# One weight load instead of two, and a last row tile that leaves in three pieces of 512, 416 and 96 columns

## The chip, the cores and the metric

The kernel runs on one core of a Trainium2 chip. The metric is the device time of one execution in microseconds (us), outside the profiler. Where the text quotes a profile, its times count from the start of the profiled execution ("span").

## The reference

A pre-norm transformer block on 2048 tokens of width 1024, in bfloat16: sliding-window attention with 32 heads and a window of 256, then a two-layer MLP with SiLU of hidden width 3584, each with a residual.

```python
h = x + attention(layernorm(x), wqkv, window=256) @ wo     # wo: 1024 x 1024
h2 = h + silu(layernorm(h) @ w1) @ w2                      # w1: 1024 x 3584, w2: 3584 x 1024
```

## The kernel before

The block is worked through in four blocks of 512 tokens. TensorE runs almost without a pause (busy for 690.1 of 695.5 us): while the scores of one block are made, it computes the projections of the next. Two places matter here. The first is where the attention output weights `wo` are loaded: into a buffer that held eight tiles of x, in two halves, at the start of the stage that projects the last block (b = 3).

```python
    r_o = big.tile([P, 8192], BF16, name="r_o")
    x_ring = [view(r_o, i * 1024, 1024) for i in range(8)]     # tiles of x, two blocks
    wo = view(r_o, 0, KT, D)                                   # the same bytes, later
    # ... for b in range(2, NB): ...
        else:                                                  # the last block
            nc.sync.dma_start(out=wo[:, 0:4, :], in_=wo_v[:, 0:4, :])
            nc.sync.dma_start(out=wo[:, 4:8, :], in_=wo_v[:, 4:8, :])
            load_res(0)
            load_res(1)
```

The second is the MLP's second matmul. Each row tile of 128 tokens is a sum over 28 tiles of the hidden width (FT = 28), in pieces of columns. Each piece has a PSUM bank, is evicted by one VectorE operation that adds the residual, and leaves by its own DMA. All row tiles have two pieces of 512 columns; the very last has four, so that little is left to do behind the last matmul.

```python
        for j in range(4):
            cols = [(0, 512), (512, 1024)]
            if b == NB - 1 and j == 3:
                cols = [(0, 512), (512, 768), (768, 896), (896, 1024)]
            accs = [next_acc() for _ in cols]
            # ...
            for acc, (c0, c1) in zip(accs, cols):
                mm2(acc, j, c0, c1, early, FT)                 # 28 matmuls
                nc.vector.scalar_tensor_tensor(out=t_out[j % 2][:, c0:c1], in0=acc[:, 0:c1 - c0], scalar=0.5,
                                               in1=t_in[j % 2][:, c0:c1], op0=ALU.mult, op1=ALU.add)
                nc.sync.dma_start(out=out2d[(b * 4 + j) * P:(b * 4 + j + 1) * P, c0:c1], in_=t_out[j % 2][:, c0:c1])
                # ... steps of the next block's layer norm in between ...
```

The softmax here doesn't subtract the row's maximum and nothing guards it: scores larger than these inputs give would overflow.

## Time and profile before

| | before |
|---|---|
| time, median of 3 (and of 6 once the change was timed) | 696.75 us (696.72 us) |
| spread of the 6 | 696.40 to 697.18 us |
| span of the profiled run | 695.5 us |
| TensorE busy | 690.1 us, 99% |
| last matmul's end to the end of the span | 2.8 us |

The lines that carry this are in the prediction. One more belongs here. It is the kernel before's list of waits in its first 8 us, and it is the first wait of the run that depends on a transfer (columns: who waits for what, us in total, times, longest):

```profile
DVE ln_st L169 <- DMA r_o<-in_A_x_dram: 2.8, 1, 2.8
```

The layer norm of the first tile cannot start before that tile is there.

### The profile page before, as it was taken

The page shows a single profiled execution, that of the slowest core. Times are in us where ns is not written, and L with a number is a line of the kernel's source. Part 1 is how long each engine was busy: PE and PEld are TensorE (multiplying, and loading weights), DVE is VectorE, ACT ScalarE, POOL GpSimd, SP SyncE. Part 2 cuts the span into 40 slices and gives each one's busy share as a digit, 9 for nine tenths or more (in the row PEclk, how much of TensorE's full clock was granted, in tenths as well). Part 3 has the DMA queues.
Part 4 walks back from the last instruction along what each step waited for, and adds up shares of the span by engine and source line. Part 5 has one row for each costly group of instructions (what it writes and reads, how often), then busy time and mean ns, then how long its engine had stood idle before and what let it go on. Part 6 is the DMA issues. An engine that isn't in the chain of part 4 may idle for free.

```text
span 695.5 us, 12334 instructions
## 1 busy us (share of the span) xinstructions
PE 690.1 (99%) x5091; PEld 331.6 (48%) x5091; DVE 289.5 (42%) x616; ACT 257.9 (37%) x328; POOL 174.5 (25%) x391
## 2 busy tenths in 40 slices
PE   8999999999999999999999999999999999999998
PEld 3444444555555555544444444444444444444445
DVE  6267646644443448544316134433133251244111
ACT  4326657777777777621310023300033100233000
POOL 1007667777777777500000000000000000000000
PEclk9999999999999999999999999999999999999999
DMA  7732131026231778880123410024200023100110
GB/s 241 257 53 77 35 93 51 17 60 193 70 124 23 205 251 272 199 311 31 31 76 99 107 38 1 1 83 77 83 1 1 11 95 91 45 1 1 30 39 24
DMA packets 76457, 60.84 MB, mean 87 GB/s; under 512 B 50288, under 2 KB 60528, under 8 KB 76400
## 3 DMA queue, kind: packets, MB, share of 16 engines
q1 hardware_dynamic: 76256, 59.78, 29.9%
q8 instruction: 40, 0.66, 0.4%
q10 hardware_dynamic: 144, 0.26, 0.1%
q14 instruction: 17, 0.14, 0.1%
HBM read 39.85 MB, written 8.39 MB: 69 GB/s over the span
## 4 chain that ended last, share of the span: by engine, by line
PE 99%; DMA 1%; DVE 0%; issue 0%
PE hacc L563 19%; PE hacc L600 17%; PE acc L248 16%; PE acc L600 10%; PE acc L563 9%; PE acc L238 8%; PE acc L267 7%; PE o_ps L339 4%; PE sc L285 3%; PE hacc L267 1%; PE o_ps L354 1%; PE sc L313 1%; DMA r_o<-in_A_x_dram 1%; PE tp L216 0%; DVE ln_st L169 0%; DVE r_o L197 0%
## 5 line engine op out<-in xcount | busy, mean ns | idle before, releaser
L330 POOL TENSOR_SCALAR_AFFINE_SELECT r_e<-r_e 128x256 bf16<-128x256 bf16 (+1 forms) x384 | 171.6, 477 | 116.5 <-ACT r_e L322 65.1
L293 ACT ACTIVATE r_e<-sc 128x1024 bf16<-128x1024 f32 x144 | 139.5, 1021 | 45.1 <-PE sc L285 31.0
L600 PEld LDWEIGHTS <-r_a 128*128 128x128 bf16 x952 | 90.9, 98 | 103.0
L563 PEld LDWEIGHTS <-r_w 128*128 128x128 bf16 x896 | 87.4, 98 | 104.8
L600 PE MATMUL hacc<-r_a 128*128 128x512 bf16 (+2 forms) x616 | 122.5, 360 | 0.0
L563 PE MATMUL hacc<-r_e,r_w 128*128 128x512 bf16 x456 | 100.9, 379 | 0.0
L572 ACT ACTIVATE r_n<-hacc 128x512 f32<-128x512 f32 x30 | 17.9, 597 | 178.9 <-PE hacc L563 178.9
L600 PE MATMUL acc<-r_a 128*128 128x512 bf16 x336 | 74.0, 379 | 0.0
L248 PEld LDWEIGHTS <-r_w 128*128 128x128 bf16 x512 | 46.5, 97 | 57.1 <-issue 7.0
L250 DVE CAST r_a<-acc 128x512 bf16<-128x512 f32 x56 | 38.7, 691 | 72.9 <-PE acc L248 56.3
L248 PE MATMUL acc<-r_t,r_w 128*128 128x512 bf16 x256 | 60.0, 379 | 0.0
L248 PE MATMUL acc<-r_w 128*128 128x512 bf16 x256 | 58.2, 380 | 0.0
L267 PE MATMUL acc<-r_o,r_a 128*128 128x512 bf16 x208 | 49.4, 380 | 0.0
L563 PE MATMUL acc<-r_e,r_w 128*128 128x512 bf16 x216 | 49.1, 379 | 0.0
L339 PEld LDWEIGHTS <-r_e 128*128 128x128 bf16 x1152 | 39.5, 96 | 17.0
L322 ACT ACTIVATE r_e<-sc 128x1024 bf16<-128x1024 f32 x36 | 34.9, 1021 | 21.2 <-PE sc L313 20.1
L339 PE MATMUL o_ps<-r_a,r_e 128*128 128x33 bf16 x1152 | 40.2, 178 | 0.0
L615 DVE SCALAR_TENSOR_TENSOR r_t<-hacc,r_t 128x512 bf16<-128x512 f32 (+2 forms) x22 | 14.0, 635 | 56.7 <-PE hacc L600 56.7
L267 PEld LDWEIGHTS <-r_a 128*128 128x128 bf16 x256 | 23.1, 98 | 29.6 <-issue 5.1
L615 DVE SCALAR_TENSOR_TENSOR r_t<-acc,r_t 128x512 bf16<-128x512 f32 x12 | 8.3, 692 | 64.2 <-PE acc L600 64.2
L573 DVE SCALAR_TENSOR_TENSOR r_a<-r_n,hacc 128x512 bf16<-128x512 f32 x30 | 20.6, 688 | 33.0 <-ACT r_n L572 33.0
L563 PE MATMUL hacc<-r_a,r_w 128*128 128x512 bf16 x144 | 32.9, 379 | 0.0
(71 smaller groups left out, 476.5 us busy)
## 6 DMA issues: line engine op xcount, KB each, us to landing
r_w<-in_B_w_dram SPq DMA_DIRECT2D x8, 896.0 KB, 5.1
r_a<-in_B_w_dram SPq DMA_DIRECT2D x7, 1024.0 KB, 7.9
r_w<-in_A_wqkv_dram SPq DMA_DIRECT2D x6, 1024.0 KB, 8.7
h_dram<-r_t SPq DMA_DIRECT2D x16, 256.0 KB, 3.0
r_t<-h_dram SPq DMA_DIRECT2D x16, 256.0 KB, 2.8
out_dram<-r_t SPq DMA_DIRECT2D x31, 128.0 KB, 1.7
r_o<-in_A_x_dram SPq DMA_DIRECT2D x15, 256.0 KB, 4.0
r_e<-h_dram SPq DMA_DIRECT2D x3, 1024.0 KB, 5.7
```

Source lines behind the costliest of these rows:

```text
L238: nc.tensor.matmul(acc, lhsT=lnT_b[b % 2][:, kt, j * P:(j + 1) * P], rhs=wv[:, kt, c * 512:(c + 1) * 512], start=(kt == 0), stop=(kt == KT ...
L248: nc.tensor.matmul(acc, lhsT=wqk[:, kt, col0:col0 + P], rhs=lnT_b[b % 2][:, kt, :], start=(kt == 0), stop=(kt == KT - 1))
L250: copy(out=(qT, kT)[which][b][:, g, :], in_=acc)
L267: nc.tensor.matmul(acc, lhsT=qT[b][:, g, j * P:(j + 1) * P], rhs=wo[:, g, c * 512:(c + 1) * 512], start=(g == 0), stop=(g == G - 1))
L285: nc.tensor.matmul(sc[hh // 2][:, hh % 2, ch * P:(ch + nq) * P], lhsT=kT[t // 4][r0:r0 + DH, g, (t % 4) * P:(t % 4 + 1) * P], rhs=qT[b][r0 ...
L293: nc.scalar.activation(out=e, in_=sc[pair], func=ACT.Exp, scale=scale)
L322: nc.scalar.activation(out=e, in_=sc[pair], func=ACT.Exp, scale=scale)
L330: nc.gpsimd.affine_select(out=ap, in_=ap, pattern=[[0, 2], [0, n], [sgn, P]], compare_op=ALU.is_ge if upper else ALU.is_gt, fill=0.0, base ...
L339: nc.tensor.matmul(o_ps[pair][:, qt * 2 + hh, 0:VW], lhsT=e_of(i, kind, pair)[:, hh, ch * P:(ch + 1) * P], rhs=v[:, b * 4 + kt, g * 4 + pa ...
L563: nc.tensor.matmul(acc, lhsT=w1[:, kt, ft * P:(ft + 1) * P], rhs=ln2T[b][:, kt, :], start=(kt == 0), stop=(kt == KT - 1))
L600: nc.tensor.matmul(acc[:, 0:c1 - c0], lhsT=gT[:, ft, j * P:(j + 1) * P], rhs=w2[ft // 4][:, ft % 4, c0:c1], start=(ft == 0), stop=(ft == F ...
L615: nc.vector.scalar_tensor_tensor(out=t_out[j % 2][:, c0:c1], in0=acc[:, 0:c1 - c0], scalar=0.5, in1=t_in[j % 2][:, c0:c1], op0=ALU.mult, o ...
```

## The change

The intent is one DMA issue less for the weights and, at the end, one piece less, with a smaller last piece.

```diff
-            nc.sync.dma_start(out=wo[:, 0:4, :], in_=wo_v[:, 0:4, :])
-            nc.sync.dma_start(out=wo[:, 4:8, :], in_=wo_v[:, 4:8, :])
+            nc.sync.dma_start(out=wo, in_=wo_v)
@@
             if b == NB - 1 and j == 3:
-                cols = [(0, 512), (512, 768), (768, 896), (896, 1024)]
+                cols = [(0, 512), (512, 928), (928, 1024)]
```

## The prediction

Passages that rested on something else than the traces of this case are cut out of the prediction and of two expectations, at the marks. No term of the prediction's sum is among them: 0.07 + 0.03 + 0.01 = 0.11 us. Three numbers need their source named. The 1.19 us of the last piece are 28 x (96 x 0.415 + 2.5) ns, from the two values worked out there. The "6.1 us with 56 matmuls" are the 6.20 us of the chain less 0.07. The "0.1 to 0.2 us" for a last transfer at double cost is an estimate; the DMA view of the kernel before from 692.5 us on shows the engines busy for 0.5, 0.8 and 0.5 of three slices of 75 ns in this transfer, 0.14 us.

> **What bounds the kernel now.** I read the page's first lines, then its chain that ended last, then the last twenty microseconds by window, by chain and by group, and last the stretch where the attention output weights are loaded.
>
> The page, its span, its first row of busy time and the summary of its chain:
>
> ```profile
> span 695.5 us, 12334 instructions
> PE 690.1 (99%) x5091; PEld 331.6 (48%) x5091; DVE 289.5 (42%) x616; ACT 257.9 (37%) x328; POOL 174.5 (25%) x391
> ...
> PE 99%; DMA 1%; DVE 0%; issue 0%
> ```
>
> The reader is to see one bound: TensorE is busy for 690.1 of 695.5 us and the chain runs over it for 99% of the span. A change elsewhere counts only if it makes TensorE wait, or if it shortens what stands before its first or behind its last matmul. The time outside the profile is 696.75 us, 1.25 us above the profiled span; I carry differences of the span over to it.
>
> The end of the run, in windows cut at the starts of the VectorE operations that evict each piece of the last row tile (512, 256, 128, 128 columns), then what is left. The columns are PE, PEld, DVE, ACT and POOL busy time, granted clock, DMA share and GB/s:
>
> ```profile
> 680.45:686.46 6.01, 6.01 (x30) 2.80 (x29) 0.69 (x1) 0.00 (x0) 0.00 (x0) 1.00 0.06 22
> 686.46:689.55 3.09, 3.09 (x32) 2.79 (x31) 0.69 (x1) 0.00 (x0) 0.00 (x0) 1.00 0.13 45
> 689.55:691.11 1.56, 1.56 (x32) 1.56 (x30) 0.42 (x1) 0.00 (x0) 0.00 (x0) 1.00 0.14 41
> 691.11:692.68 1.57, 1.53 (x28) 1.35 (x25) 0.30 (x2) 0.00 (x0) 0.00 (x0) 1.00 0.15 31
> 692.68:695.50 2.82, 0.00 (x0) 0.00 (x0) 0.29 (x1) 0.00 (x0) 0.00 (x0) 0.87 0.07 12
> ```
>
> Each piece is 28 matmuls (one for each of the 28 tiles of the hidden width); the extra ones in a window's count overlap its edges. TensorE has no gap up to 692.65 us, and then 2.8 us pass without it: one eviction, one DMA issue, one landing and the end of the program. The chain of this stretch in order of time, and the last issue in the timeline:
>
> ```profile
> 686.46 6.20 PE hacc L600 x84
> 692.65 0.02 issue
> 692.68 0.29 DVE r_t L615
> ```
>
> ```profile
> 693.00 0.36 SPq L617 DMA_DIRECT2D out_dram<-r_t  x1
> ```
>
> The evictions by width, in the groups of this stretch (mean ns of one after the bar):
>
> ```profile
> L615 DVE SCALAR_TENSOR_TENSOR r_t<-hacc,r_t 128x512 bf16<-128x512 f32 x1 | 0.7, 692 | 5.4 <-PE hacc L600 5.4
> L615 DVE SCALAR_TENSOR_TENSOR r_t<-hacc,r_t 128x128 bf16<-128x128 f32 x2 | 0.6, 292 | 2.4 <-PE hacc L600 2.4
> L615 DVE SCALAR_TENSOR_TENSOR r_t<-hacc,r_t 128x256 bf16<-128x256 f32 x1 | 0.4, 425 | 2.4 <-PE hacc L600 2.4
> ```
>
> The weights' two loads, in the timeline of the DMA queue, and the first matmul that reads them, in the timeline of all engines:
>
> ```profile
> 163.86 0.58 SPq L496 DMA_DIRECT2D r_o<-in_A_wo_dram  x1
> 165.97 0.39 SPq L497 DMA_DIRECT2D r_o<-in_A_wo_dram  x1
> 166.42 0.96 SPq L256 DMA_DIRECT2D r_a<-in_A_x_dram  x2
> 168.95 8.86 SPq L375 DMA_TRANSPOSE r_a<-r_n  x2
> ```
>
> ```profile
> 229.58 1.68 PE L267 MATMUL acc<-r_o,r_a 128*128 128x512 bf16 x7
> ```
>
> The per-line view gives 5.5 us to landing for the first half and 6.4 us for the second, so the weights are in place at 172.4 us, 57 us before they are used.
>
> [...] 1.56 us / 28 = 55.7 ns at 128 columns [...], 6.01 / 28 = 215 ns at 512 [...]. [...] the timeline has 15 matmuls of 33 columns in 0.53 us, of which 0.178 is the length of the last, so 0.35 / 14 = 25 ns, with a weight load for each. [...] The last piece has 256 B a row now and will have 192 B; the trace shows what 256 B rows cost at this place: 1.5 us from the last issue to its landing, the same 1.5 us as the 64 KB piece with 512 B rows.
>
> **The change part by part.**
>
> *Last row tile, TensorE.* The columns stay 1024, so streaming is the same; what goes is one piece, 28 weight loads and 28 matmuls, and with each matmul its fixed part. From the windows: (215 - 55.7) / 384 = 0.415 ns a column, so the fixed part is 55.7 - 128 x 0.415 = 2.5 ns. 28 x 2.5 = 0.07 us. [...] All of it is on the path: I take 0.07.
>
> *Last eviction.* 425 - 292 = 133 ns for 128 columns and 692 - 425 = 267 for 256: 1.04 ns a column and 158 ns fixed. At 96 columns this is 258 ns against 292: 0.03 us, on the path. The eviction at 416 columns takes 158 + 433 = 0.59 us and lies beside the 1.19 us of the last piece's matmuls. Its DMA issue (0.34 us) follows; 0.59 + 0.34 = 0.93 is still under 1.19 + 0.26 = 1.45, when the last issue is due. So the bigger middle piece stays hidden.
>
> *Last transfer.* 24 KB in place of 32 KB, the same 128 rows. Issue and landing are mostly fixed (1.5 us for 32 KB and for 64 KB), so I count 0.01 us. One eviction and one DMA issue less earlier on are off the path. What follows the landing stays, about 1 us (695.5 - 693.00 - 1.5).
>
> *Attention output weights.* The upper half already waits for the turned input tiles (1.4 us of wait for those transposes in the queue's view); the lower half goes 2.1 us earlier because its part of the buffer is free. In the changed order the one load stands where the first stood and carries the waits of both, so it issues at about 166 us. 2 MB now start there where 1 MB did. The halves took 5.5 and 6.4 us beside other traffic, so the load should land by 173 to 176 us, 50 us or more ahead of use at 229.58. The two residual loads and the next transposes sit behind up to 3 us more of data. The residual tiles are first used at 230 us too; the transposes write operands of that same later stage, and their source is one of three buffers that come round every 7.6 us, so they have over 10 us. SP saves one issue, 0.4 us of an engine that mostly waits. Worth: 0.00.
>
> Sum: 0.07 + 0.03 + 0.01 = 0.11 us of 696.75, or 0.016%. 696.75 - 0.11 = 696.64, which I state as 696.65.
>
> **The rivals.**
>
> *The last transfer gets worse.* Rows of 192 B that begin 1,856 B into a row of the output might cost more than aligned 256 B. [...] Against: 256 B and 512 B rows landed after the same 1.5 us. [...] even at double cost this is an estimated 0.1 to 0.2 us, and would give 696.7 to 696.8: the gain is eaten.
>
> *Something in the way of the last transfer.* The third piece took 2.6 us to land where the last took 1.5; an instruction fetch of 16 KB stood in a DMA queue in that window. Should such a fetch meet the last piece, the end moves by 1.1 us, to 697.7. With 56 TensorE instructions fewer I expect that fetch to fall away instead, with no effect on the end.
>
> *The weights' load delays something on the path.* If the transposes behind it came late enough for VectorE to wait for its buffer, TensorE would stall once by some microseconds: 698 to 700. Against: 10 us of slack by the count above, and no TensorE wait for a DMA in that stage.
>
> *The merged load helps.* One large load instead of two[...]. But TensorE has no wait there to give back: 0.
>
> **Range and chances.** Three runs of before spread over 0.43 us, four times the predicted gain, so the range is that of the runs: 696.65 with some 0.5 us to either side, 696.1 to 697.2. Two per cent are 14 us; faster by that is excluded by what stands outside TensorE's work (some 5 us in all), and slower would need a stall that nothing here suggests: 0.005, 0.99, 0.005.
>
> **What would show it.** The TensorE piece after the 512 columns lasts 6.1 us with 56 matmuls; the eviction of 96 columns takes about 258 ns and that of 416 about 590; from the last issue to the end remain 2.5 us; the load of the weights issues near 166 us, lands before 180, and no TensorE wait appears between 166 and 240 us. It would be wrong if the landing of the last piece took over 1.7 us, if VectorE or SP still held the 416 piece when the 96 columns were ready, or if transposes after 166 us held up VectorE.

## The result and the profile after

| | before | after |
|---|---|---|
| median of 6 runs | 696.72 us | 696.86 us |
| range | 696.40 to 697.18 | 696.58 to 697.20 |
| ratio, 95% interval | | 1.0001, 0.9989 to 1.0014 |
| span of the profiled run | 695.5 us | 694.9 us |

Ratios are the mean time of one kernel's fast runs over that of the other's of the same rounds, so not quite the ratio of the medians. The interval is some 0.9 us to either side; the predicted gain of 0.1 us cannot be seen in it, and neither can a loss of that size. The answer to "was the gain there?" must come from the traces.

The spans differ by 0.6 us in favour of the change, but this is not the change. In the kernel after, the same first wait reads:

```profile
DVE ln_st L169 <- DMA r_o<-in_A_x_dram: 2.3, 1, 2.3
```

and in the two timelines of VectorE, before and then after, the first statistics operation, which ends that wait, starts 0.57 us apart, before anything that was changed:

```profile
4.33 1.29 DVE L169 BATCH_NORM_STATS2 ln_st<-r_o 128x6 f32<-128x512 bf16 x2 [2.84 <-DMA r_o<-in_A_x_dram]
```

```profile
3.77 1.29 DVE L169 BATCH_NORM_STATS2 ln_st<-r_o 128x6 f32<-128x512 bf16 x2 [2.27 <-DMA r_o<-in_A_x_dram]
```

From here on I measure from the start of this operation, which takes the landing out of the comparison, and cut the rest at two events: the last DMA issue and its landing. The views print hundredths; the third decimals here are from the trace's own timestamps.

The end of the kernel after, in windows cut as before at the starts of the evictions (512, 416 and 96 columns, then the rest; columns as in the prediction):

```profile
685.92:690.84 4.92, 4.92 (x33) 2.81 (x32) 0.69 (x2) 0.00 (x0) 0.00 (x0) 1.00 0.08 27
690.84:692.03 1.19, 1.15 (x28) 1.00 (x24) 0.59 (x2) 0.00 (x0) 0.00 (x0) 1.00 0.00 0
692.03:694.90 2.87, 0.00 (x0) 0.00 (x0) 0.26 (x1) 0.00 (x0) 0.00 (x0) 1.00 0.15 46
```

Its chain in order of time, its evictions by width, and its last issue in the timeline:

```profile
685.88 6.13 PE hacc L599 x56
692.01 0.02 issue
692.03 0.26 DVE r_t L614
```

```profile
L614 DVE SCALAR_TENSOR_TENSOR r_t<-hacc,r_t 128x416 bf16<-128x416 f32 x1 | 0.6, 592 | 4.2 <-PE hacc L599 4.2
L614 DVE SCALAR_TENSOR_TENSOR r_t<-hacc,r_t 128x96 bf16<-128x96 f32 x1 | 0.3, 257 | 0.6 <-PE hacc L599 0.6
```

```profile
692.31 0.33 SPq L616 DMA_DIRECT2D out_dram<-r_t  x1
```

The pieces take 4.92 and 1.19 us (175.7 and 42.5 ns a matmul), where the prediction's 0.415 ns a column and 2.5 ns a matmul make 4.90 and 1.19; 6.13 us of TensorE in place of 6.20; 257 ns for the last eviction in place of 292. From the first statistics to the last issue: 688.661 us before, 688.548 after, 0.113 us less. The sum in the prediction up to this point was 0.10 us (0.07 + 0.03).

The load of the weights, in the timeline of the DMA queue after:

```profile
165.40 0.38 SPq L496 DMA_DIRECT2D r_o<-in_A_wo_dram  x1
```

It takes 9.5 us to land by the per-line view, so until 174.9 us.

The last transfer before and after, in the list of DMA issues (size, us from issue to landing):

```profile
out_dram<-r_t SPq DMA_DIRECT2D x1, 32.0 KB, 1.5
```

```profile
out_dram<-r_t SPq DMA_DIRECT2D x1, 24.0 KB, 1.4
```

What follows the last issue did not shrink. It took 2.49 us before and takes 2.56 after, though the landing itself got 0.05 us shorter (1.47 and 1.42 us). So of the 0.11 us gained, some 0.07 were lost again behind the last issue: 0.12 behind the landing, less the 0.05. There the prediction had said that "what follows the landing stays". The closing is a series of waits in both traces: SP passes five semaphore waits, for the same semaphores in the same order (693.40 to 694.68 us before, 692.69 to 693.78 after), then the engines drain and meet (to the end at 695.49 and 694.87 us). The per-line view of the closing has VectorE's drains (least, median and longest ns, first and last start), and the waits of SP there show how long the meeting took. First before, then after:

```profile
L648 DVEq DRAIN  x2: 19/174/330, 692.7 to 695.1; - x2
```

```profile
SPq L648 <- PEq L648: 0.6, 2, 0.4
```

```profile
L647 DVEq DRAIN  x2: 137/216/295, 692.0 to 694.5; - x2
```

```profile
SPq L647 <- PEq L647: 0.9, 2, 0.7
```

The second of VectorE's two drains is the closing one: it takes 137 ns in place of 19, and SP's longest wait in the meeting is 0.7 us in place of 0.4. In the trace this drain starts 0.44 us after the semaphore record before it, where it was 0.09 us.

Some matmul records are missing in the trace after (4976 matmuls on the page, with 5063 weight loads; the page of the kernel before has 5091 of each, 28 more). It doesn't touch these readings.

### The profile page after: what moved, and what is told of

It is laid out like the page before. It is cut to its first block, busy times and chain, and to the rows that moved or that the text cites. A ratio compares the mean times of both kernels' runs of the same rounds, so it can differ in the third digit from the quotient of the medians.

```text
span 694.9 us, 12185 instructions
## 1 busy us (share of the span) xinstructions
PE 685.5 (99%) x4976; PEld 329.8 (47%) x5063; DVE 289.3 (42%) x615; ACT 257.9 (37%) x328; POOL 174.6 (25%) x391
## 4 chain that ended last, share of the span: by engine, by line
PE 99%; issue 1%; DVE 0%
PE hacc L562 18%; PE hacc L599 17%; PE acc L248 16%; PE acc L599 10%; PE acc L562 9%; PE acc L238 8%; PE acc L267 7%; PE o_ps L339 4%; PE sc L285 3%; PE hacc L267 1%; PE o_ps L354 1%; PE sc L313 1%; PE o_ps L165 1%; PE tp L216 0%; DVE r_e L160 0%
## 5 line engine op out<-in xcount | busy, mean ns | idle before, releaser
L599 PEld LDWEIGHTS <-r_a 128*128 128x128 bf16 x924 | 89.0, 98 | 104.8
L248 PE MATMUL acc<-r_t,r_w 128*128 128x512 bf16 x241 | 58.5, 379 | 0.8
L267 PEld LDWEIGHTS <-r_a 128*128 128x128 bf16 x256 | 23.1, 98 | 29.6 <-issue 5.1
```

Of the source, the lines that this page charges most:

```text
L248: nc.tensor.matmul(acc, lhsT=wqk[:, kt, col0:col0 + P], rhs=lnT_b[b % 2][:, kt, :], start=(kt == 0), stop=(kt == KT - 1))
L267: nc.tensor.matmul(acc, lhsT=qT[b][:, g, j * P:(j + 1) * P], rhs=wo[:, g, c * 512:(c + 1) * 512], start=(g == 0), stop=(g == G - 1))
L599: nc.tensor.matmul(acc[:, 0:c1 - c0], lhsT=gT[:, ft, j * P:(j + 1) * P], rhs=w2[ft // 4][:, ft % 4, c0:c1], start=(ft == 0), stop=(ft == F ...
```

## The experiments

Theory A: the terms of the prediction hold up to the last issue, and single runs differ by the landing of the first tile. Theory B: something in the change, not chance (theory C), delays the closing. I read from each trace: first statistics to last issue; issue to landing; landing to the end of the program; and the number of VectorE's records (operations, semaphore records and drains). All in one table, the runs follow one by one. "Late" means that VectorE's closing drain took 136 to 138 ns; in all other traces it took 19. The experiments ran on three chips; wo_at_20, on another one than tail_only, repeats its stretch up to the last issue to the hundredth.

| run | to the last issue | to landing | to the end | VectorE records | drain | ratio to before (95%) |
|---|---|---|---|---|---|---|
| before | 688.66 | 1.47 | 1.02 | 707 | | |
| after | 688.55 | 1.42 | 1.14 | 705 | late | 1.0001 (0.9989 to 1.0014) |
| same_again | 688.55 | 1.43 | 1.13 | 705 | late | 0.9999 (0.9987 to 1.0012) |
| dve_pad | 688.56 | 1.43 | 0.84 | 706 | | 0.9996 (0.9983 to 1.0008) |
| tail_only | 688.54 | 1.44 | 0.96 | 706 | | 0.9997 (0.9983 to 1.0011) |
| wo_only | 688.64 | 1.46 | 0.94 | 706 | | 0.9996 (0.9983 to 1.0008) |
| dve_pad_64 | 688.56 | 1.43 | 0.84 | 765 | | 0.9994 (0.9979 to 1.0009) |
| dve_pad_128 | 688.57 | 1.42 | 0.85 | 829 | | 1.0003 (0.9987 to 1.0020) |
| dve_pad_132 | 689.82 | 1.43 | 1.14 | 833 | late | 1.0003 (0.9986 to 1.0019) |
| eighths | 708.30 | 1.45 | 0.97 | 858 | | 1.0260 (1.0244 to 1.0276) |
| two_pieces | 688.91 | 1.67 | 0.98 | 704 | | 1.0001 (0.9986 to 1.0016) |
| last32 | 688.93 | 1.46 | 1.13 | 705 | late | 1.0008 (0.9993 to 1.0023) |
| wo_at_20 | 688.54 | 1.43 | 0.84 | 706 | | 0.9998 (0.9983 to 1.0013) |
| wo_at_23 | 692.90 | 1.43 | 1.14 | 705 | late | 1.0047 (1.0030 to 1.0063) |

### same_again: the changed kernel once more

No edit.

> The changed kernel once more, unaltered. Theory A (the change is worth 0.11 us up to the last DMA issue; differences of some tenths between single runs come from when the first input tile lands, since the two traces so far differ by 0.57 us there already): from the first layer-norm statistics operation to the last DMA issue 688.55 us again (the kernel before: 688.66), whatever the start is; time within 0.3 us of the kernel before, ratio 0.9995 to 1.0005. Theory B (something in the change costs as much as it gains, since the medians show 696.86 against 696.72): the stretch up to the last issue repeats, and from the last issue to the end of the program takes 2.56 us again, against 2.49 before. Theory C (the closing stretch is chance): this stretch takes another value between 2.3 and 2.7 us.

The first statistics started at 4.40 us this time (3.77 in the trace before it), and everything behind repeated: 688.55 us to the last issue, 2.56 us from there to the end, the drain 138 ns. Its five runs have a median of 696.87 against 696.90 for the kernel before. Theory A holds, and of the other two theory B: the slow closing repeats and is not chance.

### dve_pad: one VectorE instruction more

```diff
     run_late()
     load_w2(5)
+    pad = const.tile([P, 1], F32, name="pad")
+    nc.vector.memset(pad[:], 0.0)
```

> The changed kernel with one tiny VectorE memset (128x1) ahead of the MLP, so that VectorE has as many instructions as in the kernel before (563; the change has 562). In the trace of the changed kernel VectorE's closing drain came 0.4 us after its release and took 137 ns, in the kernel before 0.09 us and 19 ns. If the late drain comes from where VectorE's instruction stream ends (theory B), it is gone here, and from the last issue to the end take about 2.2 us: 2.49 less some 0.2 because the last-landing piece is now also the last one waited for, less some 0.05 for the landing. If it is chance (theory C), this stretch bears no relation to the count. Up to the last issue 688.55 us, as theory A has it. Time: 0.3 us under the changed kernel for theory B, the same for theory C; either is at the edge of the noise.

From the last issue to the end 2.27 us, with the drain on time; the expected value was about 2.2. The per-line view of the closing and the waits of SP:

```profile
L649 DVEq DRAIN  x2: 19/158/297, 692.1 to 694.2; - x2
```

```profile
SPq L649 <- PEq L649: 0.6, 2, 0.4
```

One instruction that does nothing useful took 0.29 us off the closing. The rest of the difference to before (1.02 to 0.84 us behind the landing) has the reason that the expectation gave: SP passes five closing waits, and each one that is already met takes it 0.06 us (in the kernel before the last three start at 694.53, 694.59 and 694.65 us). In the kernel before the last landing ends the second of them, so three follow; in tail_only and wo_only the third; in this kernel and the changed one the fifth. Which one it is goes with the number of DMAs in the program: one DMA less in each part of the change, two in all. In the traces before and after, the DMAs signal eight semaphores in turn; the last of 186 signals one that SP's second closing wait asks for, the last of 184 one of the fifth. I read this order in the traces and did not vary it by itself.

### tail_only and wo_only: one part of the change each

tail_only is the kernel before with the three pieces alone, wo_only the kernel before with the single load alone.

> The kernel before with the last row tile in three pieces alone; the weights in two loads. Theory A: the whole gain is here: 688.55 us from the first statistics to the last issue, as in the changed kernel. Rival (merging the loads gave part of the 0.11 us): 688.6 or more. Time within 0.3 us of the kernel before.

> The kernel before with the single weight load alone; the last tile in four pieces. Theory A: nothing: 688.66 us from the first statistics to the last issue, as in the kernel before; the load issues near 166 us and lands before 176. Rival: any difference of 0.03 us or more there would be the merged load's. From the last issue to the end 2.49 us as before if that stretch depends on the program (it has before's VectorE count and tail), other values if it is chance.

688.54 us and 688.64 us to the last issue: the gain of 0.11 us is in the tail, and wo_only is only 0.02 us under the kernel before, below the 0.03 us that I had set as the least to be called a difference. The single load in wo_only was issued at 165.6 us and landed 9.5 us later.

The closing is quick in both, 2.40 us from issue to end. For wo_only I had expected 2.49 as before; most of the difference is the one closing wait fewer behind the last landing. For tail_only it is a surprise, since its trace has as many VectorE operations as the changed kernel's (615; the kernel before has 616; the 562 and 563 in the expectation of dve_pad stand in no trace). So my explanation by the count of operations needed a correction: what counts are all records. The tail removes one eviction (707 to 706), the merged load one semaphore record of VectorE's (707 to 706), and only both together reach 705, where the drain is late. Neither part alone has the loss.

### dve_pad_64, dve_pad_128 and dve_pad_132: does 705 come round?

The expectation of the first two was that 128 more instructions would bring the late drain back and 64 would not. The 128 was my estimate; no trace up to then showed it.

```diff
             silu(b, acc, ft)
+            if 1 <= b <= 2 or b == 3 and ft < 8:
+                nc.vector.memset(pad[:], 0.0)          # 64 in all; twice each for 128
```

> The changed kernel with 64 tiny VectorE memsets spread over the MLP. What is to be told apart: the closing drain of VectorE was late (137 ns, some 0.35 us after it was due) in both traces with 705 VectorE records and in none with 706 or 707. Theory B (the late drain belongs to a place in the instruction stream that comes round with the 8 KB instruction fetches[...]): with 769 records it is not late, and from the last issue to the end take 2.27 us as with one memset. Theory B' (what matters is only having more instructions than 705): the same here. Up to the last issue 688.55 us in either; a slower MLP would show that the memsets themselves cost something.

> The same with 128 memsets, 833 VectorE records if none is added beside them. Theory B (period of 128): the closing drain is late again and from the last issue to the end take 2.56 us. Theory B': not late, 2.27 us. Theory C (chance): either. Up to the last issue 688.55 us.

Neither was late, but the second did not test what it was meant to. Four semaphore records fell away where the memsets were put, so it had 829 records and not 833. With four memsets more at the last of these places:

> The changed kernel with 132 tiny VectorE memsets in the MLP. The run with 128 of them gave 829 VectorE records and not the 833 (705 + 128) that its expectation named, as four semaphore records fell away (with 64 memsets, too: 765); so the period of 128 has not been tried. This one should have 833. The late closing drain came in all four traces with 705 records and in none with 704, 706, 707, 765, 829 or 858. Theory B (a place in the stream that comes round every 128 instructions, with the 8 KB fetches): late, and from the last issue to the end 2.56 us. Theory B' (705 is late for another reason): not late, 2.27 us. Up to the last issue 688.55 us.

833 records, and the drain is late: 138 ns, 2.56 us from issue to end.

```profile
L652 DVEq DRAIN  x2: 138/218/297, 694.2 to 696.6; - x2
```

That is 705 + 128, as theory B had it. Its 689.82 us to the last issue missed the expectation by 1.3 us, and this belongs to the start of that one run: its first 15 us had a granted clock of 0.89 (0.50 from 7.8 to 11.2 us) and 11.73 us of TensorE, the changed kernel's 1.00 and 13.39. It was the slowest of its four runs (698.72 us, the others 696.47 to 697.12).

The traces have 8 KB instruction fetches (DMA queue q14 of the page: 17 packets in the kernel before, 16 in the changed one). How many instructions one of them brings is not shown.

The times of these fetches go with a place in VectorE's stream. In the nine traces with 704, 705 or 706 records the last one starts 1.11 to 1.13 us after the end of VectorE's record number 703; in dve_pad_132 it starts as long after number 831, which is 703 + 128. The record behind that place, number 704 or 832, is the late one: it starts 0.44 to 0.46 us after the one before it, where a drain in the closing is otherwise 0.09 us behind. With 705 and 833 records this is the closing drain, and the whole meeting waits for it (SP's longest wait there is 0.7 us in place of 0.4). With 704 (two_pieces) it is VectorE's very last semaphore record, which comes 0.115 us after that of SP; in all other traces it comes 0.01 us after. With 706 it is a semaphore record that starts 1.7 to 1.9 us later, when the meeting of the engines begins, so that the step is hidden.

So the place is shown, and that it comes round after 128 records by one run. What takes the time in the step is not shown: the fetch itself starts 0.53 to 0.55 us after the late drain has ended, so the drain did not wait for that fetch, and no record says what it waited for.

### eighths: the fixed cost of a matmul, made large

```diff
+            elif b > 0 or j > 0:
+                cols = [(c, c + 128) for c in range(0, D, 128)]
```

> The kernel before with 14 of the 15 row tiles of the MLP's second matmul after the first, and the last but for its own four pieces left alone, in eight pieces of 128 columns in place of two of 512; so 14 x 6 x 28 = 2352 more matmuls and weight loads over the same columns. Theory A (each matmul has a fixed 2.5 ns and its weight load is hidden): 2352 x 2.5 ns = 5.9 us more up to the last issue, 694.5 us, and a time 5.9 us over the kernel before, ratio 1.0084. [...] Rival (the fixed part is hidden or an edge effect of the last tile): under 2 us more.

The expectation failed: 19.6 us more and not 5.9 up to the last issue, and 1.026 in time. But the fixed cost itself is as expected. In the last block, where no layer norm of a next block lies between, TensorE runs on (busy for all 37 us from 660 to 697), and VectorE's timeline has a piece of 128 columns every 1.563 us (24 evictions; two of them):

```profile
690.42 0.29 DVE L617 SCALAR_TENSOR_TENSOR r_t<-acc,r_t 128x128 bf16<-128x128 f32 x1 [1.27 <-PE acc L600]
691.98 0.29 DVE L617 SCALAR_TENSOR_TENSOR r_t<-acc,r_t 128x128 bf16<-128x128 f32 x1 [1.27 <-PE acc L600]
```

1.563 us / 28 = 55.8 ns a matmul with its weight load, over 36 us; four such pieces are 0.21 us more than one of 512 columns (6.04 us), which is 84 times 2.5 ns. So 5.9 us of the 19.6 are this. The rest is something I had not looked for: the three earlier blocks. The waits of TensorE and of VectorE between 360 and 660 us:

```profile
PE hacc L600 <- DVE r_t L617: 7.6, 4, 1.9
```

```profile
DVE ln_st L169 <- DMA r_e<-h_dram: 18.2, 3, 6.3
```

The next block's layer norm stands between the evictions, and VectorE waits there up to 6.3 us for its rows to arrive from memory. With pieces of 6 us and six PSUM banks nobody notices (the kernel before has the same waits, 18.6 us in all, and TensorE does not stop); with pieces of 1.56 us the banks run out and TensorE stops, 7.6 us in all, and in the same places its granted clock is lower. Two windows of the first of the three places show it (clock third from the right: 0.97, then 0.91; in the kernel before it was 1.00 in both):

```profile
366.00:381.00 15.00, 11.21 (x193) 10.96 (x191) 8.49 (x28) 0.00 (x0) 0.00 (x0) 0.97 0.34 110
381.00:396.00 15.00, 15.00 (x249) 15.00 (x247) 5.12 (x17) 0.00 (x0) 0.00 (x0) 0.91 0.67 118
```

In the windows of the other two places, 22 us each, the clock is 0.92. Cut closer, each of the three places has one stretch of 3.41 us with a clock of 0.50 (from 380.24, 472.40 and 574.80 us). At a clock of 0.50 in dve_pad_132 seven matmuls of 512 columns took 3.09 us from 8.30 us on, 0.44 us each and not 0.216. So half of these stretches is lost, an estimated 5.1 us (3 x 3.41 / 2). With 5.9 for the matmuls and 7.6 for the waits this is 18.6 of the 19.6 us. The profiled execution was the slowest of the four (716.48 us, mean clock 0.993; the others 713.87 to 714.37 us and 0.998 to 1.000), so the clock's part must be smaller in the others, which left no trace.

### two_pieces and last32: the sizes of the last pieces

```diff
-                cols = [(0, 512), (512, 928), (928, 1024)]
+                cols = [(0, 512), (512, 1024)]               # two_pieces
+                cols = [(0, 512), (512, 992), (992, 1024)]   # last32
```

> The changed kernel with the last row tile in two pieces of 512. It sizes the eviction term: theory A: TensorE saves 28 x 2.5 ns = 0.07 us, the last eviction takes 692 ns in place of 257, so the last issue comes 0.37 us later: 688.91 us from the first statistics. The landing of 128 KB takes some 0.2 us more than that of 24 KB (1.7 against 1.43). In all about 0.5 us more than the changed kernel. Rival (the last eviction is hidden): 688.5.

> The changed kernel with last pieces of 480 and 32 columns in place of 416 and 96. Theory A with the floor (25 ns from matmul to matmul, seen with 33 columns): 28 x 202.5 ns + 28 x 25 ns = 6.37 us of TensorE in place of 6.11, so the last eviction starts 6.37 + 0.03 us after the eviction of the 512 piece starts. Without a floor: 28 x 15.8 = 0.44 us and 6.11 + 0.03. The middle eviction, 0.66 us, and its DMA issue, 0.33 us, should now hold up SP: last issue 6.7 to 6.8 us after the eviction of the 512 piece in place of 6.39, that is 688.9 us from the first statistics.

two_pieces: 688.91 us, as expected, so the last eviction is on the path at its full length. The landing of its 128 KB took 1.67 us against 1.43 for 24 KB. From the last issue to the end it needs 2.65 us: with 704 records its drain is on time, and only the last semaphore record, as said above, is some 0.1 us late.

last32: the windows from the eviction of the 512 piece to that of the 480 piece, then to that of the 32 piece:

```profile
686.08:691.75 5.67, 5.67 (x36) 2.84 (x35) 0.69 (x1) 0.00 (x0) 0.00 (x0) 1.00 0.07 23
691.75:692.44 0.69, 0.66 (x27) 0.55 (x23) 0.66 (x1) 0.00 (x0) 0.00 (x0) 1.00 0.00 0
```

0.69 us / 28 = 25 ns a matmul, the same as the prediction read from 33 columns. The 15.8 ns of the expectation without a floor, and its 202.5 ns for 480 columns, are 0.417 ns a column and 2.5 ns a matmul, from 215.8 ns at 512 columns (6.04 us / 28) and 55.8 ns at 128 (eighths); at 480 columns that held (5.67 us / 28 = 202.5 ns), at 32 it did not. The last issue comes 6.78 us after the eviction of the 512 piece (6.40 in the changed kernel), of which 0.2 us is SP still busy with the middle piece's DMA. This smaller last piece is worse by 0.38 us: 96 columns took 42.5 ns a matmul, as the columns and the fixed part have it, and their 1.19 us left SP time. Sizes between 32 and 96 were not tried.

### wo_at_20 and wo_at_23: how much slack the load has

The load moved from the start of its stage into the loop, to the iterations n = 20 and n = 23 of 24.

```diff
-            nc.sync.dma_start(out=wo, in_=wo_v)
@@
+                if b == NB - 1 and n == 20:      # or 23
+                    nc.sync.dma_start(out=wo, in_=wo_v)
                 scores(b - 1, g, kind)
```

> The changed kernel with the weights' load moved from about 166 us to about 218 us, 11 us ahead of its first use. Theory A (the load has over 50 us of slack, so that merging and the 2 us later start cannot matter): it lands by 227 us, TensorE waits for nothing, and 688.55 us up to the last issue. Rival (the place of the load in the queue matters, through the transposes and residual loads behind it): more than 688.6.

> The same, moved to about 226 us, 3 us ahead of the first use. Theory A: the load lands 6 to 8 us after its issue, so TensorE waits 3 to 5 us for it near 229 us, and the whole run is longer by that: 691.5 to 693.5 us up to the last issue, ratio 1.004 to 1.007. If TensorE waits for it and the end doesn't move, the slack is not where I think it is.

At n = 20 it was issued at 215.8 us, landed at 225.3, and nothing moved: 688.54 us. (This kernel happens to have 706 records and a quick closing.) Both issues came 2 us earlier than the expectations said, and the landings took 8.4 to 9.5 us where the second one said 6 to 8. At n = 23 it was issued at 223.7 us and landed at 232.1, and TensorE waited for it. The waits of TensorE's weight loads there, and the window behind:

```profile
PEld L267 <- DMA r_t<-in_A_x_dram: 3.0, 1, 3.0
```

```profile
229.00:236.00 7.00, 4.26 (x41) 1.79 (x41) 1.29 (x4) 1.94 (x2) 3.11 (x7) 0.76 1.07 375
```

The view names another transfer that landed at about the same time; the load moved is the only thing that was changed, and its landing at 232.1 is where TensorE starts again (232.2). TensorE's own wait is 2.7 us (3.0 for its weight loads). From 232.0 to 235.4 us its granted clock was 0.50, an estimated 1.7 us of work lost (half of 3.4). Together this is 4.4 us, and the last issue is 4.35 us later. So the slack in the prediction is real: issued 50 us later the load costs nothing, issued 58 us later it makes TensorE wait for 3. Merging the loads, which moves the start by about 2 us, cannot be felt.

No kernel here beats the kernels before and after by a margin that the times show. By the traces wo_at_20, dve_pad_64 and dve_pad are the best, within 0.02 us of each other (0.32 to 0.34 us under before and 0.27 to 0.29 under after, from the first statistics to the end). Their ratios, 0.9994 to 0.9998, fit that but do not prove it.

## Why the prediction was right or wrong, point by point

- The time, 696.86 us, lies in the range of 696.1 to 697.2 and 0.2 us from the predicted 696.65. That closeness is luck in part, as the spread between runs is larger and 0.07 us of the gain were lost in a way not foreseen; and it is no proof of a gain of 0.1 us: the interval of the ratio reaches nine times as far to either side.
- TensorE's term, 0.07 us, and the eviction's, 0.03 us: right. 0.113 us measured up to the last issue, 688.54 to 688.57 us in the seven traces with this tail and an undisturbed start, tail_only among them. eighths shows the 2.5 ns over 672 matmuls in a row.
- The middle piece stays hidden: right at 416 columns (SP was free when the last issue was due), and last32 shows where it stops being right.
- The last transfer: 0.01 us expected, 0.05 us measured. The rival that rows of 192 B would cost more is refuted: 1.42 us for 24 KB in rows of 192 B, 1.47 us for 32 KB in rows of 256 B. The one with an instruction fetch in its way did not come about: the 16 KB instruction fetches on the page (queue q8) went from 40 to 39, as expected, and the middle piece landed in 1.7 us where the third one before had taken 2.6.
- The weights: worth nothing, right; issued at 165.4 us and landed at 174.9, within what was said, with the slack measured by wo_at_20 and wo_at_23. The rival that it delays something is refuted: the transposes issued next landed at 176.7 us (174.8 before), and from 166 to 240 us neither TensorE nor VectorE waits for a transfer.
- "What follows the landing stays, about 1 us": this step failed, by an amount that the range covers. It went from 1.02 to 1.14 us. Two things in it, neither considered: three closing waits of 0.06 us fewer behind the last landing, and 0.29 us more because VectorE's stream now ends so that its closing drain is record number 704, the late one. Only both parts of the change together bring it there.
- Two readings in the prediction are off and change nothing in its result. Its first window ends at 686.46 us, but the eviction there starts at 686.49 in the timeline. Cut at that point, the 512 piece takes 6.04 us, 215.8 ns a matmul, and the 256 piece 3.06; the fixed part then comes out at 2.5 ns, where the prediction's own 55.7 - 128 x 0.415 is 2.6. And its 1.25 us between time and span pairs the median of three with the span of another execution: the profiled one took 697.29 us, 1.8 us above its span, and the one after 696.59, 1.7 us above.
- The spread between runs: taken as given in the prediction. The traces show a source: the first statistics began between 3.41 and 4.61 us in the fourteen traces, ahead of all that was changed.

## What to carry to other kernels

TensorE was busy here for 690.1 of 695.5 us, and the change at the tail was worth what it took off TensorE's last pieces and the last eviction: 0.113 us up to the last DMA issue, where 0.10 had been worked out from durations in the trace. The timing of whole runs did not show it; its interval was 0.9 us to either side. Measure such a change from an event after the first landing to the last issue, and look at the closing separately: the mere number of DMAs and instructions moved it by as much as 0.3 us here (0.84 to 1.14 us behind the landing), more than the change was worth. Before cutting pieces finer, ask which waits the long pieces were hiding: 18.6 us of VectorE's here, and in eighths they stopped TensorE for 7.6 us in all.
